# Attention with plain float32 products on parts of the array, in a pipeline one step deeper

## The chip, the cores and the metric

The kernel runs on one core of one Trainium2 chip, and the metric is the device time of one execution in microseconds (us). One core has five engines that run side by side, each through its own instructions in order: TensorE (PE; its weight loads are shown apart, as PEld), VectorE (DVE), ScalarE (ACT), GpSimd (POOL), and SyncE (SP), which issues this kernel's DMAs. [...]

## What is computed

The reference is an attention layer followed by two feed-forward layers. Only the attention is touched by the change:

```python
# q_l, k_l, v_l: 4 batches x 8 heads x 512 x 64;  q_g, k_g, v_g: 4 x 8 x 32 x 64
out_g = softmax(scale * q_g @ [k_g, k_l].T) @ [v_g, v_l]       # 32 global rows see all 544 keys
s_lg  = scale * q_l @ k_g.T                                    # local rows see the 32 global keys
s_ll  = where(abs(i - j) <= 32, scale * q_l @ k_l.T, -1e9)     # and a window of local keys
out_l = softmax([s_lg, s_ll]) @ [v_g, v_l]
...   # then x (2176 tokens x 512) through a feed-forward layer and a mixture of 8 experts
```

## The kernel before

The attention works on 16 *items*; an item is one batch and one pair of heads, so its 2 x 64 head columns fill the 128 partitions. An item has two *local steps* (`l`, two blocks of 128 queries each); after every second item comes one *global step* (`g`, the 4 x 32 global queries of two items). So five steps form a group, l l l l g, and there are 8 groups and 40 steps. A local block sees a segment of 224 keys: its own 128, the 32 global ones, and 32 from either neighbour (`SEG`).

Products are made with two float32r numbers for each float32 number: a rounded part (`hi`) and the rest (`lo`). `split_terms` makes three products of them, hi·hi, hi·lo and lo·hi, and PE adds them up in PSUM. So every operand must be split: a value leaves PSUM by an ACT copy that rounds (`hi`), and then a DVE subtraction that leaves the rest (`lo`). That is `evacuate_all` (L549 to L560).

A step goes through these pieces. `loc_scores` or `glob_scores` (PE, into two PSUM banks `s`); `loc_least` (DVE adds the mask and finds the least, from `s` to `e`) or `glob_least`; `loc_exp` or `glob_exp` (ACT; the global one reads the banks `s` themselves); `loc_normalise` (DVE reciprocal, then POOL scales `e`); `loc_transpose` or `glob_transpose` (PE turns `e` into `pta` and `ptb`), evacuated as `ah`, `al`, `bh`, `bl`; `loc_values` or `glob_values` (PE, into `pv`), evacuated into `xh`, `xl`, the input of the next layer. A global result is first scaled and picked from `pv` by four small operations (`pick`), then turned once more (`turn`).

The loop at L856 is a software pipeline written by hand, and nothing reorders it. Iteration k emits: least of step k-1, evacuation of what PE left in iteration k-1, exponentials of k-1, **values of k-4, scores of k, transposes of k-2**, then turns and the next item's `prep_qk`. Each engine gets its share of that in this order.

Operands of an item: `prep_qk` turns the raw keys and queries on PE and evacuates them to `kt` and `q`. `prep_edges` copies the neighbours' 32 columns and the global keys into `kt` by DMA (4 DMAs) and loads a later item's raw keys and queries (4 DMAs). `prep_v` splits the raw values on POOL (`split_pool`, L270) into `va`, copies edges and global values into `vb` by DMA (4 DMAs), and loads a later item's values (2 DMAs). `glob_queries` spreads the global queries with POOL copies into a block-diagonal tile `bd`, so that one 128-wide product makes the scores of two heads, the other head's rows being zeros.

During the attention `step_side` splits the first weights of the next layer on ACT, DVE and POOL, and after the last step `step_early` puts that layer's first products (L435) between the attention's last steps. From there to the end PE runs the feed-forward products (L435, L1078, L1331, L1404, L1570).

## Time and profile before

| | us |
|---|---|
| median of 3 runs (lowest, highest) | 1963.38 (1962.86, 1964.88) |
| the profiled execution, and its span | 1959.21, 1957.3 |
| PE busy | 1928.7 (99%) |
| DVE, ACT, POOL busy | 1443.9 (74%), 995.9 (51%), 581.4 (30%) |
| chain that ended last | PE 90%, DVE 3%, ACT 2%, DMA 2% |
| scores of the first and the last global step start | 23.95, 180.27 |
| first product of the next layer's second half (L1078) starts | 204.51 |

Busy shares over the whole span are those of the feed-forward layers, which last from about 205 us to the end. The attention is its first tenth, with other shares, so it has to be read by itself: in stretches from one global step to the next, and within such a stretch in the rows in order of time. A PE row's duration overlaps its neighbours' (products are pipelined), so what a block of PE work costs is read from start to start, not from durations. DMA-issuing instructions are not counted as busy.

### The profile page before, as it was taken

How to read it: one execution, taken by the hardware profiler on the slowest of the kernel's cores; microseconds unless marked ns; L12 is line 12 of the kernel's file. 1: busy time of each engine (PE TensorE's matmuls, PEld its weight loads, DVE VectorE, ACT ScalarE, POOL GpSimd, SP SyncE). 2: the span in 40 equal slices, each digit the busy share in tenths (PEclk: the TensorE clock that was granted, in tenths of full speed). 3: DMA queues.
4: the chain of work that ended last, by engine and by line, in shares of the span. 5: the costliest groups of instructions: out<-in, count | busy, mean ns of one | idle time of the engine just before them, and what ended most of it. 6: DMA issues, size and time to landing. Idle time of an engine off the chain costs nothing.

```text
span 1957.3 us, 34874 instructions
## 1 busy us (share of the span) xinstructions
PE 1928.7 (99%) x12482; PEld 1833.6 (94%) x12482; DVE 1443.9 (74%) x3075; ACT 995.9 (51%) x2325; POOL 581.4 (30%) x673
## 2 busy tenths in 40 slices
PE   9999999999999999999999999999999999999998
PEld 7888988989898899999999999999999999999998
DVE  7998575755359888888886776776777776767867
ACT  7988533323245555545554454454455454554543
POOL 6555431323126554555421101211103101111010
PEclk9999999999999999999999999999999999999999
DMA  7665220211016999998997667667676776676674
GB/s 163 139 144 133 66 65 22 65 44 49 28 32 224 308 302 301 306 301 299 311 329 269 211 224 250 214 237 244 206 260 213 248 249 236 207 258 225 208 267 141
DMA packets 359294, 391.34 MB, mean 200 GB/s; under 512 B 114256, under 2 KB 240208, under 8 KB 359120
## 3 DMA queue, kind: packets, MB, share of 16 engines
q1 hardware_dynamic: 359120, 389.10, 61.1%
q8 instruction: 99, 1.62, 0.3%
q14 instruction: 75, 0.61, 0.1%
HBM read 281.82 MB, written 96.73 MB: 193 GB/s over the span
## 4 chain that ended last, share of the span: by engine, by line
PE 90%; DVE 3%; ACT 2%; DMA 2%; SPq 1%; POOL 1%; issue 1%; DVEq 0%; POOLq 0%; ACTq 0%
PE z L1570 14%; PE a L1331 14%; PE y L1404 11%; PE h L435 10%; PE y L1078 9%; PE d L1570 7%; PE d L1331 7%; PE pa L1331 5%; PE b L1570 4%; PE b L1331 3%; PE pd L1331 2%; PE pb L1331 1%; PE pv L723 1%; ACT e L682 1%; DMA w2forms<-w 1%
## 5 line engine op out<-in xcount | busy, mean ns | idle before, releaser
L1202 POOL TENSOR_TENSOR w<-raw,w 128x256 fp32r<-128x256 f32 (+1 forms) x124 | 122.9, 1023 | 774.0 <-ACT w L1198 697.8
L1331 PE MATMUL a<-xh,w 128*128 128x384 f32 x1024 | 286.0, 335 | 0.0
L1543 ACT CAST xh<-wide 128x384 fp32r<-128x384 f32 x384 | 189.2, 512 | 112.9 <-PE d L1570 95.2
L1547 DVE TENSOR_TENSOR xl<-wide,xh 128x384 fp32r<-128x384 f32 x384 | 200.4, 549 | 24.7 <-ACT xh L1543 24.5
L1532 ACT COPY snaps<-a 128x384 f32<-128x384 f32 x128 | 61.3, 480 | 296.2 <-PE a L1331 224.8
L1404 PE MATMUL y<-w,xh 128*128 128x512 f32 x640 | 197.9, 390 | 0.7 <-ACT xh L1388 0.7
L1078 PE MATMUL y<-hid,w 128*128 128x384 f32 (+1 forms) x960 | 191.7, 356 | 0.0
L1584 DVE SCALAR_TENSOR_TENSOR acc<-z,prob,acc 128x256 f32<-128x256 f32 x366 | 162.0, 475 | 38.8 <-PE z L1570 38.7
L1331 PEld LDWEIGHTS a<-xh,w 128*128 128x128 f32 x1024 | 187.6, 188 | 0.0
L1078 PEld LDWEIGHTS y<-hid,w 128*128 128x128 f32 x960 | 171.9, 188 | 14.9
L435 PE MATMUL h<-xh,w 128*128 128x384 f32 (+1 forms) x640 | 182.6, 358 | 0.0
L1331 PE MATMUL a<-xl,w 128*128 128x384 f32 x512 | 171.2, 334 | 0.0
L1536 DVE TENSOR_TENSOR wide<-b,snaps 128x384 f32<-128x384 f32 x64 | 35.7, 557 | 157.9 <-PE b L1331 156.1
L1331 PE MATMUL d<-xh,w 128*128 128x384 f32 x512 | 150.5, 334 | 0.0
L441 ACT ACTIVATE r<-h 128x384 f32<-128x384 f32 (+1 forms) x76 | 40.4, 532 | 203.3 <-PE h L435 200.4
L1552 DVE TENSOR_TENSOR wide<-wide 128x384 f32<-128x384 f32 x256 | 138.8, 551 | 5.9 <-ACT wide L1540 0.8
L1404 PEld LDWEIGHTS y<-w,xh 128*128 128x128 f32 x640 | 119.2, 188 | 24.8 <-ACT xh L1388 1.1
L435 PEld LDWEIGHTS h<-xh,w 128*128 128x128 f32 x640 | 117.8, 188 | 13.3 <-issue 3.2
L1331 PE MATMUL pa<-xh,w 128*128 128x320 f32 x512 | 128.8, 310 | 1.0 <-ACT snaps L1366 0.6
L1404 PE MATMUL y<-w,xl 128*128 128x512 f32 x320 | 124.7, 390 | 0.9 <-DVE xl L1393 0.9
L1570 PE MATMUL z<-wf,xh 128*128 128x256 f32 x768 | 123.5, 283 | 0.0
L1540 ACT ACTIVATE wide<-wide 128x384 f32<-128x384 f32 x192 | 101.3, 528 | 33.0 <-DVE wide L1536 33.0
(255 smaller groups left out, 5073.4 us busy)
## 6 DMA issues: line engine op xcount, KB each, us to landing
raw<-in_moe_w_dram SPq DMA_DIRECT2D x128, 512.0 KB, 5.7
w<-w1forms SPq DMA_DIRECT2D x256, 256.0 KB, 4.9
w<-w2forms SPq DMA_DIRECT2D x256, 256.0 KB, 5.3
wf<-w2forms SPq DMA_DIRECT2D x192, 256.0 KB, 5.6
w1forms<-w SPq DMA_DIRECT2D x128, 256.0 KB, 4.2
w2forms<-w SPq DMA_DIRECT2D x192, 128.0 KB, 3.2
w2forms<-xl SPq DMA_DIRECT2D x64, 256.0 KB, 4.9
w2forms<-xh SPq DMA_DIRECT2D x64, 256.0 KB, 3.9
```

The costliest lines, as they stand in the source:

```text
L435: nc.tensor.matmul(ps, lhsT=w, rhs=x, start=(k == 0), stop=(k == 3 * NC - 1))
L1078: nc.tensor.matmul(ps, lhsT=w, rhs=m, start=(f == 0 and x == 0), stop=(f == last and x == 2))
L1202: eng.tensor_tensor(out=lo, in0=src, in1=f32(hi), op=ALU.subtract)
L1331: nc.tensor.matmul(ps, lhsT=lhs, rhs=rhs, start=(first and t == 0), stop=(t == 5), skip_group_check=True)
L1404: nc.tensor.matmul(y[t0], lhsT=lhs, rhs=rhs, start=(t == 0), stop=(t == 3 * UF - 1))
L1532: act.copy(snap[{"1": "p1", "5": "p5" + q, "6": "u2" + q}[i]], bank(("d" if i == "5" else "a") + q)[:, 0:n])
L1540: act.activation(out=dst, in_=bank("a" + q)[:, 0:n] if name == "A21" else dst, func=AF.Relu)
L1543: act.copy(hidden_form(name, 0, int(q)), h[HOME[name]][int(q)])
L1547: dve.tensor_tensor(out=hidden_form(name, 1, q), in0=h[HOME[name]][q], in1=f32(hidden_form(name, 0, q)), op=sub)
L1552: dve.tensor_tensor(out=x, in0=x, in1=h[other][int(q)], op=op)
L1570: nc.tensor.matmul(ps, lhsT=lhs, rhs=rhs, start=(form in ("B11", "T1") and x == 0), stop=(x == 5), skip_group_check=True)
L1584: dve.scalar_tensor_tensor(out=dst, in0=width(t, src), scalar=pr, in1=dst, op0=mul, op1=add)
```

## The change

The operands are no longer split. `kt`, `q`, `va`, `vb`, `kg`, `qg`, `vg`, `gz` and the turned probabilities (`pa`, `pb`) hold plain float32, once. PE multiplies float32 by float32, one product where there were three, and each product uses a part of the array: local scores 64 rows (as before), local values 64 columns for either head, global scores 64 rows by 32 columns, global values 32 columns. `bd` and `glob_queries` go. Values are loaded by DMA straight into `va` (two tiles for eight items each), so `split_pool` goes from `prep_v`. Copies out of PSUM are given to ACT (`"a"`) or DVE (`"v"`); only `xh`, `xl` are still split. Steps are pipelined one deeper: scores of k, values of k-5, transposes of k-3, with seven iterations after the last step instead of six.

```diff
@@ storage
-        ap3 = actx.enter_context(tc.tile_pool(name="ap3", bufs=3))
+        ap3 = actx.enter_context(tc.tile_pool(name="ap3", bufs=4))
...
+        KT = [ap1.tile([P, NQ, SEG], F32, name=f"kt{i}") for i in range(3)]
+        VA = [share.tile([P, 2, NQ, 2, P], F32, tag=f"va{i}", name=f"va{i}") for i in range(2)]
+        VB = [ap1.tile([P, NQ, P], F32, name=f"vb{i}")[0:96] for i in range(3)]
...
         def load_v(n):
...
-            r = stage.tile([P, 2, NQ, 2, D], F32, tag="r1", name="rv")[:, 0]
-            load_pair(r, v_l, b, p)
-            rawv[n] = r
+            load_pair(values_of(n).rearrange("p t (h d) -> p t h d", h=2), v_l, b, p)
@@ evacuate_all
+            for eng, hi, lo, ps, scale in waiting:
+                if eng == "a":
...
+            for eng, hi, lo, ps, scale in waiting:
+                if lo is not None:
                     nc.vector.tensor_tensor(out=lo, in0=ps, in1=f32(hi), op=ALU.subtract)
-                else:
-                    nc.vector.scalar_tensor_tensor(out=lo, in0=ps, scalar=scale, in1=f32(hi), op0=ALU.mult, op1=ALU.subtract)
+                elif eng == "v":
+                    if scale == 1.0:
+                        nc.vector.tensor_copy(hi, ps)
+                    else:
+                        nc.vector.tensor_scalar(out=hi, in0=ps, scalar1=scale, scalar2=None, op0=ALU.mult)
@@ prep_qk
-            evacuate((kt[:, 0, :, 0:P], kt[:, 1, :, 0:P], trk, 1.0))
+            evacuate(("v", kt[:, :, 0:P], None, trk, 1.0))
...
+            evacuate(("a" if n == 0 else "v", q, None, trq, QSCALE))
@@ prep_edges
-                nc.sync.dma_start(out=flat[:, 1:, 160:192], in_=flat[:, :-1, P - WINDOW : P])
-                nc.sync.dma_start(out=flat[:, :-1, 192:224], in_=flat[:, 1:, 0:WINDOW])
-                for x in range(2):
-                    nc.sync.dma_start(out=f32(kt[:, x, :, P : P + SG]), in_=keys[x])
+                nc.sync.dma_start(out=kt[:, 1:, 160:192], in_=kt[:, :-1, P - WINDOW : P])
+                nc.sync.dma_start(out=kt[:, :-1, 192:224], in_=kt[:, 1:, 0:WINDOW])
+                nc.sync.dma_start(out=kt[:, :, P : P + SG], in_=keys)
@@ prep_v
-            split_pool(va[:, 0], va[:, 1], r.rearrange("p t h d -> p t (h d)"))
...
-            for x in range(2):
-                g = vg[b * SG : (b + 1) * SG, x, p * P : (p + 1) * P]
-                nc.sync.dma_start(out=f32(vb[0:SG, x]), in_=f32(g).unsqueeze(1).to_broadcast([SG, NQ, P]))
+            g = vg[b * SG : (b + 1) * SG, p * P : (p + 1) * P]
+            nc.sync.dma_start(out=vb[0:SG], in_=g.unsqueeze(1).to_broadcast([SG, NQ, P]))
@@ loc_scores
+                for s, r in zip(s_t[i], halves):
+                    nc.tensor.matmul(s[:, t, :], lhsT=q[r, qt], rhs=kt[r, qt], start=True, stop=True)
@@ loc_transpose
-            evacuate((ah, al, pa.rearrange("p t j q -> p t (j q)"), 1.0), (bh, bl, pb[0:96].rearrange("p t j q -> p t (j q)"), 1.0))
+            evacuate(("a", a, None, pa, 1.0), ("v", c, None, pb[0:96], 1.0))
@@ loc_values
+            pv = pss.tile([P, 2, P], F32, tag="pv", name="pv")
...
+                for x, (v, e) in enumerate(zip(sources, pt)):
+                    for j, r in enumerate(halves):
+                        nc.tensor.matmul(pv[r, t], lhsT=v[:, qt, r], rhs=e[:, t, j], start=(x == 0), stop=(x == 1))
...
+            evacuate(("a", part(xh), part(xl), pv, 1.0))
@@ glob_scores
+            for x, (out, cols) in enumerate(((sa, lambda k: k[:, 0, 0 : P + SG]), (sb, lambda k: k[:, 1:NQ, 0:P]))):
+                for j, r in enumerate(halves):
+                    for y in range(2):
+                        g = slice((2 * j + y) * SG, (2 * j + y + 1) * SG)
+                        w = qg[r, p - 1 + y, b * SG : (b + 1) * SG]
+                        nc.tensor.matmul(out[g], lhsT=w, rhs=cols(KT[(n - 1 + y) % 3][r]), start=True, stop=True)
@@ glob_values
+            pv = pss.tile([P, D], F32, tag="pv", name="pv")
+            for c in range(NQ + 1):
+                for j, r in enumerate(halves):
+                    for y in range(2):
+                        g = slice((2 * j + y) * SG, (2 * j + y + 1) * SG)
...
+                        nc.tensor.matmul(pv[g], lhsT=w, rhs=v, start=(c == 0), stop=(c == NQ))
...
             def pick():
...
+                nc.vector.tensor_scalar(
+                    out=own.rearrange("p (j d) -> p j d", j=2), in0=src, scalar1=inv[:, 0:1], scalar2=None, op0=ALU.mult
+                )
@@ the loop
-        for k in range(len(steps) + 6):
+        for k in range(len(steps) + 7):
...
-            at(k - 4, loc_values, glob_values, 1)
             at(k, loc_scores, glob_scores, 1)
...
-            at(k - 2, lambda i, n, qp: loc_transpose(i), glob_transpose, 1)
+            at(k - 5, loc_values, glob_values, 1)
+            at(k - 3, lambda i, n, qp: loc_transpose(i), glob_transpose, 1)
...
-                split_pool(vg[:, 0], vg[:, 1], graw["v"])
...
-                if n % 2:
-                    glob_queries(n)
```

What that does to the order is shown at three places. On PE, a local step's iteration with a global step's transposes, before: the last two of twelve value products (L723), scores (L660), transposes (L781, L786), then the next item's keys and queries (L575, L578).

```order
L723 MATMUL pv<-bl,vb_96 128x256
L723 MATMUL pv<-bh,vb_96 128x256
L660 MATMUL s<-kt_94,q 128x224 x12
L781 MATMUL pta<-ident,e 128x128 x4
L786 MATMUL ptb<-ident,e 128x128
L575 MATMUL trk<-ident,rqk 128x128 x4
L578 MATMUL trq<-ident,rqk 128x128 x4
```

The same on PE with the change; L642 are the scores, L702 the values, L750 and L755 the transposes.

```order
L642 MATMUL s<-kt_92,q 128x224 x4
L702 MATMUL pv<-pa,va_95 64x128 x2
L702 MATMUL pv<-pb,vb_98 64x128 x2
L702 MATMUL pv<-pa,va_95 64x128 x2
L702 MATMUL pv<-pb,vb_98 64x128 x2
L750 MATMUL pta<-ident,e 128x128 x4
L755 MATMUL ptb<-ident,e 128x128
```

The scores are four products of 224 columns instead of twelve, the values eight of 128 columns instead of twelve of 256, and the values now stand behind the scores.

On ACT, the iteration that handles a global step's exponentials (L763, L764), before; L552 and L554 are evacuations.

```order
L552 CAST xh<-pv 64x256 x2
L552 CAST ah<-pta 128x512
L552 CAST bh<-ptb 96x512
L552 CAST xh<-pv 64x2x32 x2
L552 CAST kt_93<-trk 128x4x128
L554 ACTIVATE q<-trq 128x512
L763 ACTIVATE e,st<-s,st 128x160
L764 ACTIVATE e,st<-s,st 128x384
```

The same place on ACT with the change, and the iteration behind it.

```order
L551 COPY pa<-pta 128x512
L732 ACTIVATE e,st<-s,st 128x160
L733 ACTIVATE e,st<-s,st 128x384
L551 CAST xh<-pv 128x256
L551 COPY pa<-pta 128x512
L551 CAST xh<-pv 64x2x32 x2
L664 ACTIVATE e,st<-e,st 128x224 x4
L667 ACTIVATE st<-st 128x4
```

One copy stands ahead of the global exponentials instead of seven; those of `ptb`, `kt` and `q` are now DVE's, and the small ones of the turned global result have moved one iteration on.

On SP, the DMAs of one item in the steady state, before: edges and global values into `vb`, raw values, edges and global keys into `kt`, raw keys and queries.

```order
L629 DMA vb_96<-va 32x7x128
L630 DMA vb_96<-va 32x7x128
L633 DMA vb_96<-vg 32x4x128 x2
L467 DMA rv<-in_v_l_dram 128x4x64 x2
L606 DMA kt_92<-kt_92 128x7x32
L607 DMA kt_92<-kt_92 128x7x32
L609 DMA kt_92<-kg 128x4x32 x2
```

The same on SP with the change.

```order
L620 DMA vb_98<-va_96 32x3x128
L621 DMA vb_98<-va_96 32x3x128
L623 DMA vb_98<-vg 32x4x128
L467 DMA va_96<-in_v_l_dram 128x4x64 x2
L605 DMA kt_92<-kt_92 128x3x32
L606 DMA kt_92<-kt_92 128x3x32
L607 DMA kt_92<-kg 128x4x32
```

With the four loads of raw keys and queries an item has 12 DMAs instead of 14, the edge copies move 3 blocks instead of 7, and raw values go to `va` itself.

## Rows read from the trace of the kernel before

**Rows 1.** Busy time by stretch; borders are global steps' first scores (us).

```profile
core 0: us, PE busy (x) PEld busy (x) DVE busy (x) ACT busy (x) POOL busy (x), PEclk, DMA share, GB/s
23.95:44.20 20.25, 19.73 (x178) 18.25 (x177) 18.36 (x67) 18.99 (x65) 10.97 (x23) 1.00 0.73 150
...
156.56:180.27 23.71, 21.03 (x170) 18.02 (x170) 21.57 (x66) 20.51 (x67) 15.03 (x28) 1.00 0.53 127
180.27:204.51 24.24, 23.69 (x135) 20.97 (x136) 15.27 (x39) 14.13 (x40) 9.99 (x14) 0.93 0.25 81
```

**Rows 2.** PE in order of time: start, us, line, out<-in, shape, count.

```profile
101.56 0.60 PE L575 MATMUL trk<-ident,rqk 128*128 128x128 f32 x4
...
102.35 0.36 PE L723 MATMUL pv<-ah,va 128*128 128x256 f32 x1
...
103.95 0.93 PE L660 MATMUL s<-kt,q 64*128 64x224 f32 x12
104.81 0.66 PE L706 MATMUL pta<-ident,e 128*128 128x128 f32 x4
...
105.66 0.48 PE L803 MATMUL pv<-va,ah 128*128 128x256 f32 x2
...
107.61 0.93 PE L660 MATMUL s<-kt,q 64*128 64x224 f32 x12
...
111.05 0.34 PE L746 MATMUL s<-kt,bd 128*128 128x160 f32 x1
...
112.88 0.66 PE L706 MATMUL pta<-ident,e 128*128 128x128 f32 x4
```

**Rows 3.** PE in order of time, around the gate's plain float32 products (L982).

```profile
504.56 1.06 PE L982 MATMUL lt<-acc,gt 128*32 128x512 f32 x8
505.55 0.50 PE L435 MATMUL h<-xh,w 128*128 128x512 f32 x1
...
563.65 0.85 PE L982 MATMUL lt<-acc,gt 128*32 128x384 f32 x8
564.44 0.45 PE L435 MATMUL h<-xh,w 128*128 128x384 f32 x1
```

**Rows 4.** ACT by line, 23.95 to 180.27 us: xcount | busy, mean ns | idle before.

```profile
L552 ACT CAST ah<-pta 128x512 fp32r<-128x512 f32 x35 | 20.5, 586 | 9.9 <-PE pta L706 8.1 <-PE pta L781 1.3
L552 ACT CAST xh<-pv 64x256 fp32r<-64x256 f32 x56 | 20.2, 361 | 0.7 <-PE pv L723 0.3
L552 ACT CAST bh<-ptb 96x512 fp32r<-96x512 f32 x29 | 17.0, 585 | 0.0
...
L764 ACT ACTIVATE e<-s,st 128x384 f32<-128x384 f32 x7 | 4.1, 591 | 0.0
L763 ACT ACTIVATE e<-s,st 128x160 f32<-128x160 f32 x7 | 2.8, 398 | 0.0
```

**Rows 5.** DVE by line, the same stretch.

```profile
L557 DVE TENSOR_TENSOR al<-pta,ah 128x512 fp32r<-128x512 f32 x35 | 24.2, 691 | 1.1
L557 DVE TENSOR_TENSOR xl<-pv,xh 64x256 fp32r<-64x256 f32 x56 | 23.5, 419 | 1.6 <-ACT xh L552 1.2
```

**Rows 6.** SP's DMA issues in order of time, first and last of one item's.

```profile
114.99 0.92 SPq L467 DMA_DIRECT2D rqk<-in_k_l_dram  x2
...
122.48 1.35 SPq L609 DMA_DIRECT2D kt<-kg  x2
```

**Rows 7.** PE's longest waits, 23.95 to 180.27 us: total, times, longest.

```profile
PE pv L723 <- DMA vb<-vg: 3.1, 5, 1.4
...
PE s L660 <- ACT e L764: 1.4, 7, 0.2
```

**Rows 8.** PE in order of time, before the first global step.

```profile
16.79 1.07 PE L706 MATMUL pta<-ident,e 128*128 128x128 f32 x4
...
18.36 1.06 PE L575 MATMUL trk<-ident,rqk 128*128 128x128 f32 x4
...
22.42 0.36 PE L723 MATMUL pv<-ah,va 128*128 128x256 f32 x1
```

More of the change, by code (lines that the diff above doesn't have):

```diff
@@ L655, in loc_scores @@
                 qt = 2 * qp + t
-                pairs = [split_terms(q[r, 0, qt], q[r, 1, qt], kt[r, 0, qt], kt[r, 1, qt]) for r in halves]
-                for x in range(3):
-                    for s, terms in zip(s_t[i], pairs):
-                        a, c = terms[x]
-                        nc.tensor.matmul(s[:, t, :], lhsT=a, rhs=c, start=(x == 0), stop=(x == 2))
+                for s, r in zip(s_t[i], halves):
+                    nc.tensor.matmul(s[:, t, :], lhsT=q[r, qt], rhs=kt[r, qt], start=True, stop=True)
         def loc_least(i, n, qp, between):
@@ L804, in glob_values @@
             own = OG[n // 2 % 2]
             def pick():
-                for h in range(4):
-                    r = slice(h * SG, (h + 1) * SG)
-                    dst = own[r, h % 2 * D : (h % 2 + 1) * D]
-                    if h < 2:
-                        nc.scalar.activation(out=dst, in_=pv[r, h, :], func=AF.Copy, scale=inv[r, 0:1])
-                    else:
-                        nc.vector.tensor_scalar(out=dst, in0=pv[r, h, :], scalar1=inv[r, 0:1], scalar2=None, op0=ALU.mult)
+                src = pv.unsqueeze(1).to_broadcast([P, 2, D])
@@ L815, in turn @@
+                nc.vector.tensor_scalar(
+                    out=own.rearrange("p (j d) -> p j d", j=2), in0=src, scalar1=inv[:, 0:1], scalar2=None, op0=ALU.mult
+                )
             def turn():
                 ps = pss.tile([P, 2, 2, SG], F32, tag="pv", name="pv")
-                nc.tensor.transpose(ps.rearrange("p i j q -> p (i j q)"), own, ident)
+                nc.tensor.transpose(ps.rearrange("p j i q -> p (j i q)"), own, ident)
                 c0 = GL + b * SG
                 part = lambda x, r: x[r, p - 1 : p + 1, c0 : c0 + SG]
-                evacuate(*((part(xh, r), part(xl, r), ps[r, :, j, :], 1.0) for j, r in enumerate(halves)))
+                evacuate(*(("a", part(xh, r), part(xl, r), ps[r, j], 1.0) for j, r in enumerate(halves)))
```

139 lines of the change are left out of this document (48 added, 91 removed).

## The prediction

> **What bounds the kernel now.** I read the profile in this order. First the page: over the whole span PE is busy 99% and holds 90% of the chain that ended last, but these are the feed-forward layers, which the change doesn't touch. They begin at about 205 us and take the rest. So only the attention can give or take time, and what ends it earlier ends everything earlier, as long as PE stays full behind it. Then busy time by stretch, cut at the global steps [rows 1]: from the first global scores at 23.95 to the last at 180.27 us there are seven groups of five steps, (180.27 - 23.95) / 7 = **22.33 us a group**; the shortest has 20.25, the longest 23.71. In each, PE, DVE and ACT are all busy some 18 to 21.6 us. No engine alone sets the pace. [...]
>
> Last, PE in order of time, from block start to block start [rows 2]: preparing an item 102.35 - 101.56 = 0.79, local values 1.60, local scores 0.86, local transposes 0.85, global values 107.61 - 105.66 = 1.95, global scores 112.88 - 111.05 = 1.83. Eight transposes in 0.85 make 0.106 each; a global step has five and a turn, 0.64. A group has four local steps and two items: 4 x (0.86 + 1.60 + 0.85) + 2 x 0.79 + 1.83 + 1.95 + 0.64 = **19.2 us of PE work**. So PE waits 1.0 us in the shortest group and 3.1 in the mean one: for edge DMAs, for the exponentials of a global step [rows 7], for POOL and DVE.
>
> **PE after the change.** The price of plain float32 on parts of the array is in the trace already: the gate at L982 multiplies four products of 128 rows by 32 columns, side by side on the array (recorded as eight, two passes each). With 512 moving columns the block takes 505.55 - 504.56 = 0.99 us, with 384 it takes 0.79 [rows 3]. [...] The fixed part is 0.99 - 512 x 0.00156 = 0.19 us, in which the change of array layout on either side is included. So a block costs 0.19 + 0.00156 x (columns that one part has to take in series):
> - local scores, two halves abreast, 2 x 224 columns: 0.89;
> - local values, two halves abreast, 2 blocks x 2 sources x 128: 0.99;
> - global scores, four parts abreast, 160 + 384: 1.04;
> - global values, four abreast, 5 x 64: 0.69.
>
> These are chains of more and shorter pieces than the gate's; I round up to 0.95, 1.10, 1.10 and 0.85. [...] A group is then 4 x (0.95 + 1.10 + 0.85) + 2 x 0.79 + 1.10 + 0.85 + 0.64 = **15.8 us**, 3.4 less. Scores become no cheaper; values do.
>
> **ACT and DVE.** Per group ACT loses four `bh` (0.585), half of eight `xh` (0.361 each; one copy of 128 partitions takes as long as one of 64, by its columns), and two `kt` and two `q` (512 columns as well, so 0.59 each) [rows 4]: 2.3 + 1.4 + 2.4 = 6.1 off about 19.8, the mean of the two groups in [rows 1], so 13.7; the small picks and `gz` go as well, not counted. DVE loses five `al` (0.691) and half of eight `xl` (0.419) [rows 5], 5.1 us off about 20.0, so 14.9, and keeps as many 512-column operations, now copies. The trace has no such DVE copy out of PSUM; it lies between ACT's 0.585 and the subtraction's 0.691, and I take 0.6, nearer to the copy: 8 x 0.08 less, so about 14.3 us. Both come to lie under PE's 15.8, while before ACT's and DVE's 20 lay above PE's 19.2. So PE becomes the bound. POOL loses the value split and `bd`; it was busy 11 to 15 us a group [rows 1] and bounds nothing.
>
> **Waits, old and new.** Transposes of k-3 come a whole iteration after POOL has scaled `e`, so that wait goes; so does the one for `bd`, and `vb` has one step more to land. What is late next: the first local scores behind a global step. They need both banks `s`, which the global exponentials read. From the global iteration's start on PE: scores 1.10, values 0.85, half the transposes 0.43, 2.4 in all; then ACT copies `pa` (0.59) and makes the two exponentials (0.40 and 0.59, with their sums some 0.2 more) [rows 4], 4.2 us. PE's own work there is 1.10 + 0.85 + 0.85 + 0.79 = 3.6, so PE waits 0.6 and some signal time, say 0.8. Queued behind the waiting scores are values and transposes, which ACT and DVE need an iteration later. After an iteration that prepares an item DVE has `kt` and `q` to copy (1.2) before its next masks, and PE's scores stand behind these: an estimate of 0.3. That is 15.8 + 1.1 = 16.9 for an undisturbed group. Before, undisturbed was 1.0 over the PE sum and the mean 3.1; with the value split off POOL I take 1.7, so **17.5 us a group** (16.8 to 18.9 by these ends).
>
> SP: before, an item's 14 issues take 8.84 us (114.99 to 123.83), 0.63 each [rows 6]; 12 make 7.6, two items 15.2 of 17.5. It fits, but barely.
>
> **Start and end.** Until the first global step, an iteration deeper means that one block of transposes (16.79 to 18.36) and one of values (22.42 to 23.95) leave the way [rows 8, 1]: 1.57 + 1.53 = 3.1 us earlier. [...]
>
> Sum: 3.1 + 7 x (22.33 - 17.5) + 2.7 = 39.6 us. The profiled execution's own time is 1959.21 (span 1957.3 and 1.9 around it), 4.2 under the median; 1959.2 - 39.6 = 1919.6, and against the median 1963.4 - 39.6 = **1923.8 us**. With 16.8 and 18.9 us a group it is 1919 and 1934.
>
> **Rivals.**
> *SP sets the pace.* Each item's `kt` issues wait until DVE has copied `kt`, and all loads queue behind them. If SP stands there 2 us an item, a group takes 2 x (7.6 + 2) = 19.2: 3.1 + 7 x 3.1 + 2.7 = 27.5 saved, 1936. For it: 12 issues leave little room. Against it: before, too, SP filled most of its time and PE waited only 3.1 us in all for edges [rows 7], and these now have a step more.
>
> *The row halves take turns at one bank.* In the global scores both row halves write the same bank `sa`, then the same `sb`; the old local scores gave each half a bank of its own, and L982 uses all rows, so no row here shows two row parts on one bank. If they alternate, global scores cost 0.19 + 0.00156 x 2 x 544 = 1.89, 0.85 more in each of eight groups, 6.8 us: 1931. [...]
>
> *Slower: the parts don't run abreast.* If float32's two passes of one part keep the other part from starting, every block pays all its columns in series: local scores 0.19 + 896 x 0.00156 = 1.59, values 1.79, global scores 3.58, global values 2.19. A group is 4 x (1.59 + 1.79 + 0.85) + 1.58 + 3.58 + 2.19 + 0.64 = 24.9, with the same 1.7 of waits 26.6: 7 x 4.3 = 30 us more, and the end 4 us longer instead of shorter: about 1994. It decides when PE's sum passes 22.33 - 1.7 = 20.6. Against it stand the gate's rows, four abreast [rows 3]; for it only that the gate's parts share their rows and these halves partly don't.
>
> *No gain:* PE waits grow by what its work shrinks, as before, when three engines were each about 90% busy. Nothing in the sums above forces it.
>
> **How the numbers follow.** Forecast 1924 with its own range 1916 to 1934: 0.60. SP or another engine's chain at 18.9 to 20 us a group, 1934 to 1946: 0.14. The shared bank, 1931: 0.10. Fewer waits still, below 1916: 0.05. No change that can be told (0.2%, about 4 us, is what a measurement of this kernel can tell): 0.03. Slower: 0.08. The range 1911 to 1945 leaves out the slower case, no change, and the ends beyond. Faster 0.89, same 0.03, slower 0.08.
>
> **What would show it.** Right: global scores follow each other every 17 to 18 us; values start about 1.1 us before transposes, halves starting in pairs; PE's waits are small and named ACT exponentials and DVE masks; DVE and ACT busy some 14 us a group, PE nearly all of it. Wrong: score or value blocks twice as long (parts in series), global scores of 1.9 us (bank), SP without a gap and PE waiting for DMAs into `kt` or `vb`, a clock below 1.00 within groups, or gaps of PE behind 205 us, if the next layer's weights aren't ready when it starts 40 us earlier.

## The result, and the profile after

The changed kernel takes **1932.06 us** (median of 4 runs, 1930.96 to 1936.96), the kernel before beside it 1963.78 (1962.86 to 1964.88). The ratio is 0.9843, 95% interval 0.9825 to 0.9861: faster by 31.7 us. The forecast was 1924, its own range 1916 to 1934, the range on record 1911 to 1945. The profiled run took 1932.42 us, of which the span is 1930.6.

The page's first part, of the changed kernel: PE is as full as before, since most of the span is the feed-forward part.

```profile
PE 1904.1 (99%) x12714; PEld 1790.2 (93%) x12714; DVE 1400.4 (73%) x2984; ACT 948.2 (49%) x2204; POOL 542.4 (28%) x605
```

Busy time by stretch, again from one step's global scores to the next, with the columns of [rows 1]; the last row runs from the last global scores to 175 us:

```profile
core 0: us, PE busy (x) PEld busy (x) DVE busy (x) ACT busy (x) POOL busy (x), PEclk, DMA share, GB/s
19.63:36.20 16.57, 16.45 (x167) 12.48 (x166) 13.20 (x54) 13.16 (x50) 6.96 (x16) 1.00 0.64 142
36.20:53.80 17.60, 16.98 (x207) 13.17 (x206) 14.03 (x58) 13.78 (x52) 6.96 (x16) 1.00 0.65 139
53.80:74.67 20.87, 18.57 (x208) 14.32 (x207) 15.34 (x60) 14.40 (x53) 7.10 (x17) 0.92 0.64 140
74.67:92.73 18.06, 17.23 (x207) 13.17 (x206) 15.36 (x60) 14.31 (x53) 9.80 (x18) 1.00 0.50 110
92.73:111.72 18.99, 17.01 (x208) 13.18 (x207) 15.32 (x60) 14.41 (x53) 7.59 (x17) 1.00 0.71 155
111.72:130.12 18.40, 17.24 (x208) 13.17 (x207) 15.41 (x60) 14.32 (x53) 9.80 (x18) 1.00 0.59 126
130.12:150.16 20.04, 17.46 (x199) 12.82 (x199) 15.93 (x62) 16.41 (x56) 9.92 (x19) 0.99 0.70 183
150.16:175.00 24.84, 24.84 (x246) 18.63 (x247) 12.02 (x30) 11.57 (x31) 10.68 (x13) 0.94 0.07 23
```

The seven groups take (150.16 - 19.63) / 7 = 18.65 us against 22.33, and range from 16.57 to 20.87. DVE and ACT have fallen from 18.4 to 21.6 us a group to 13.2 to 16.4. PE is the fullest engine in each group, as forecast, but it is not full in all: in the third group 2.3 us are idle and the clock was 0.92.

PE in order of time (start, us, line, out<-in, shape, count), to be read from block start to block start as [rows 2]:

```profile
89.72 1.03 PE L642 MATMUL s<-kt,q 64*128 64x224 f32 x8
90.68 0.44 PE L702 MATMUL pv<-pa,va 128*64 128x128 f32 x4
...
91.71 0.66 PE L686 MATMUL pta<-ident,e 128*128 128x128 f32 x4
...
92.73 1.39 PE L716 MATMUL s<-kt,qg 64*32 64x160 f32 x16
94.05 0.65 PE L772 MATMUL pv<-va,pa 128*32 128x64 f32 x32
...
94.75 0.66 PE L686 MATMUL pta<-ident,e 128*128 128x128 f32 x4
95.24 0.60 PE L689 MATMUL ptb<-ident,e 128*96 128x128 f32 x4
95.68 0.60 PE L577 MATMUL trk<-ident,rqk 128*128 128x128 f32 x4
96.11 0.60 PE L580 MATMUL trq<-ident,rqk 128*128 128x128 f32 x4
96.64 1.41 PE L642 MATMUL s<-kt,q 64*128 64x224 f32 x8
97.98 0.33 PE L702 MATMUL pv<-pa,va 128*64 128x128 f32 x2
```

Local scores (L642) 0.96 us, local values (L702) 1.03, transposes (L686, L689) 92.73 - 91.71 = 1.02 and 95.68 - 94.75 = 0.93, global scores (L716) 1.32, global values (L772) 0.70, preparing an item (L577, L580) 0.96. The scores behind a global step, at 96.64, take 1.34.

What PE waited for in these 130.5 us (total, times, longest), beside [rows 7], and the row at their end, whose wait the list leaves out:

```profile
PE s L642 <- DMA kt<-kg: 5.1, 3, 2.2
PE s L642 <- DVE pb L559: 1.1, 2, 0.6
PE s L642 <- ACT e L732: 0.4, 2, 0.2
...
150.16 2.19 PE L716 MATMUL s<-kt,qg 64*32 64x160 f32 x16 [2.28 <-DVE st L653]
```

The gate's first block, which began at 504.56 us [rows 3], begins at 473.64, 30.9 us earlier:

```profile
473.64 1.06 PE L945 MATMUL lt<-acc,gt 128*32 128x512 f32 x8
```

It comes at a fixed place in the row of PE, so it is the clock by which all kernels below are compared: what it moves, the attention has gained or lost. Behind it the profiles scatter: span minus gate start is 1957.3 - 504.56 = 1452.7 us before and 1930.6 - 473.64 = 1457.0 after, and lies between these two or up to 0.5 above in the twelve profiles of the experiments. The spans of the profiled pair differ by 26.7 us, 4.2 less than the 30.9. With one profile of the kernel before I read these 4.2 us as scatter behind the attention, since the medians differ by 31.7.

### The profile page after: what moved, and what is told of

It reads as the page before. It is cut to its first block, busy times and chain, and to the rows that moved or that the text cites. A ratio compares the mean times of both kernels' runs of the same rounds, so it can differ in the third digit from the quotient of the medians.

```text
span 1930.6 us, 34913 instructions
## 1 busy us (share of the span) xinstructions
PE 1904.1 (99%) x12714; PEld 1790.2 (93%) x12714; DVE 1400.4 (73%) x2984; ACT 948.2 (49%) x2204; POOL 542.4 (28%) x605
## 3 DMA queue, kind: packets, MB, share of 16 engines
q8 instruction: 100, 1.64, 0.3%
## 4 chain that ended last, share of the span: by engine, by line
PE 92%; DMA 3%; DVE 2%; SPq 1%; ACT 1%; issue 1%; POOL 0%; DVEq 0%; ACTq 0%
PE z L1533 14%; PE a L1294 13%; PE y L1367 10%; PE h L435 10%; PE y L1041 10%; PE d L1533 7%; PE d L1294 7%; PE pa L1294 5%; PE b L1533 4%; PE b L1294 3%; PE pd L1294 2%; PE s L642 1%; PE pb L1294 1%; PE pv L702 1%; DMA w<-w2forms 1%; PE pta L686 1%
```

## The experiments

All go with the changed kernel unless said. "Group" is the mean of the seven stretches between global scores, "gate" the start of the gate's first block in the profile. Times are medians; the interval is that of the ratio to the kernel before, run beside each. Not all kernels ran beside each other, so kernels of different rounds are to be compared by their ratios.

| kernel | us | 95% of the ratio | group | gate |
|---|---|---|---|---|
| before (profile) | 1961.6 to 1963.8 | | 22.33 | 504.56 |
| changed (profile) | 1932.06 | 0.9825 to 0.9861 | 18.65 | 473.64 |
| again | 1934.79 | 0.9840 to 0.9884 | 19.03 | 477.38 |
| weights_r1 | 1926.93 | 0.9803 to 0.9838 | 17.83 | 468.56 |
| values_queue_pool | 1931.46 | 0.9819 to 0.9852 | 18.17 | 473.46 |
| values_in_turn | 1938.20 | 0.9866 to 0.9908 | 19.66 | 481.50 |
| gscores_halves_r1 | 1927.99 | 0.9807 to 0.9836 | 18.08 | 470.04 |
| depth_4_2 | 1934.63 | 0.9833 to 0.9881 | 19.35 | 479.89 |
| depth_4_2_r1 | 1924.32 | 0.9789 to 0.9818 | 17.68 | 467.05 |
| before_depth_5_3 | 2017.09 | 1.0232 to 1.0314 | 28.75 | 550.41 |
| three_e (one run) | 1961.07 | | 22.74 | 504.05 |
| values_first_r1 | 1927.61 | 0.9802 to 0.9829 | 18.58 | 473.77 |
| values_first_r1_abs | 1922.94 | 0.9781 to 0.9808 | 17.60 | 467.19 |
| mixed_r1_abs | 1921.75 | 0.9783 to 0.9810 | 17.50 | 465.27 |

**again**: no edit.

> The changed kernel once more, with a profile of its own. In its first profile the feed-forward gave back 4.4 us of the 30.9 us that the attention had gained: the clock fell to 0.5 at 549.1 to 552.5 us behind the 1.88 us wait for DVE's acc, and two later waits were 0.5 to 0.7 us longer each. Theory: these are chance, not a consequence of the change; then this profile shows the first feed-forward product about 31 us earlier than in the kernel before, as the first one did, but the clock drop at 549 us and the longer waits need not be there, and the span may be 1926 to 1931 us. Rival: the attention's new end shifts the feed-forward's transfers against its work; then the same drop at the same place comes again, and the span is 1930 to 1931 us.

The gate moved 27.2 us this time, 30.9 in the first profile: the waits for `kt` were 6.6 us instead of 5.1, and waits for DVE's masks came to 2.4, where the first profile's list has none (2.3 more stand in both before the last global scores). So much the attention itself varies from one execution to the next; neither span that was expected came, 1933.9 was measured. The clock drop behind the 1.88 us wait is there again (0.57 over the 3 us behind it). Over all fourteen profiles it stands in nine, and not in those of the kernel before, depth_4_2, values_in_turn, values_first_r1 and mixed_r1_abs, of which four have the change's products. The stretch in which it falls, in the first profile and in that of mixed_r1_abs, each with the stretch ahead of it, in which PE is idle 3.00 - 1.12 = 1.88 us (columns as above):

```profile
546.64:549.64 3.00, 1.12 (x7) 1.07 (x6) 3.00 (x7) 1.09 (x3) 1.87 (x2) 0.92 0.00 0
549.64:552.64 3.00, 3.00 (x15) 1.50 (x14) 1.42 (x3) 2.04 (x6) 2.22 (x3) 0.52 0.84 307
```

```profile
538.27:541.27 3.00, 1.12 (x11) 0.93 (x14) 3.00 (x7) 1.09 (x3) 1.87 (x2) 1.00 0.00 0
541.27:544.27 3.00, 3.00 (x26) 2.38 (x25) 1.41 (x3) 3.00 (x9) 2.35 (x3) 1.00 0.84 307
```

It comes and goes behind the same wait, so the theory was right that the change doesn't bring it, and wrong in taking it for an exception.

**weights_r1** and **values_queue_pool**: who makes PE wait for the key edges?

```diff
-                    load_part(0, EARLY_PARTS[n], tag="r0")
+                    load_part(0, EARLY_PARTS[n], tag="r1")
```

> One edit to the changed kernel: the two early raw weight loads go into the stage buffer r1, which nothing uses by then, instead of taking one of the two r0 buffers that the raw queries and keys turn over in. Theory (buffer rotation): with r0 taken, SP waits at 54.9 and at 94.0 us until a later item's transposes have run, then issues 12 DMAs back to back, and the key edges land at 67.4 and 106.0 us, after PE wanted them; that is 2.24 and 1.92 us of PE waits for kt, and the clock drop at 67.86 us behind the first costs about 1.7 us more. Without the conflict these go: the groups that took 20.87 and 18.99 us come to about 17.5, and the kernel is 5 to 7 us faster, about 1926 us. Rival (SP's issues set the pace, 12 of some 0.63 us an item): the count is the same, the edges stay late, and the time moves by less than 1.5 us.

```diff
-        def load_pair(dst, src, b, p):
+        def load_pair(dst, src, b, p, queue=nc.sync):
...
-                nc.sync.dma_start(...)
+                queue.dma_start(...)
...
-            load_pair(values_of(n)..., v_l, b, p)
+            load_pair(values_of(n)..., v_l, b, p, nc.gpsimd if n > 1 else nc.sync)
```

> The changed kernel with the loads of the values (two DMAs an item, from the third item on) issued by POOL instead of SP; the early weight loads keep taking an r0 buffer. SP then issues 10 DMAs an item instead of 12, about 6.3 us instead of 7.6. Theory (buffer rotation): SP still stands at 54.9 and 94.0 us until a later item's transposes, but has 1.2 to 2.4 us less to issue behind it, so the kt waits (5.1 us in the first profile, 6.6 in the second) fall by about half, and the time falls by 2 to 4 us to about 1930 us, less than the r1 buffer gave (1926.9). Rival (SP's count of issues): the waits go altogether and the time falls as with the r1 buffer or more, to 1927 us or below.

SP's queue in order of time, first of the changed kernel:

```profile
54.91 0.57 SPq L361 DMA_DIRECT2D raw<-in_moe_w_in_dram  x1
57.81 0.92 SPq L467 DMA_DIRECT2D rqk<-in_k_l_dram  x2
...
63.25 1.20 SPq L605 DMA_DIRECT2D kt<-kt  x1
64.49 0.65 SPq L606 DMA_DIRECT2D kt<-kt  x1
65.18 0.63 SPq L607 DMA_DIRECT2D kt<-kg  x1
```

and the product on PE that these feed, with its wait in brackets, and the two behind it:

```profile
67.41 1.47 PE L642 MATMUL s<-kt,q 64*128 64x224 f32 x8 [2.24 <-DMA kt<-kg]
68.81 0.69 PE L702 MATMUL pv<-pa,va 128*64 128x128 f32 x4
...
70.71 0.91 PE L750 MATMUL pta<-ident,e 128*128 128x128 f32 x4
```

Between the early weight load at 54.91 and the next raw load at 57.81 SP stands still: both `r0` buffers are taken, one by the weights. The twelve issues behind run back to back, the last edge is issued at 65.18, and PE, which wanted it at 67.41 - 2.24 = 65.17, waits. Behind the wait PE's granted clock was 0.50 from 67.86 to 71.27 us: local values take 70.71 - 68.81 = 1.90 us there, not 1.03. With `r1` the same place reads:

```profile
55.03 0.63 SPq L361 DMA_DIRECT2D raw<-in_moe_w_in_dram  x1
55.76 1.00 SPq L467 DMA_DIRECT2D rqk<-in_k_l_dram  x2
...
64.45 0.59 SPq L607 DMA_DIRECT2D kt<-kg  x1
...
66.79 1.03 PE L642 MATMUL s<-kt,q 64*128 64x224 f32 x8 [1.33 <-DMA kt<-kg]
```

The stand is gone, the clock stays at 1.00, waits for `kt` fall from 5.1 (6.6) to 1.3 us, the third and fifth group from 20.87 and 18.99 to 18.12 and 17.82, and the kernel from 1934.8 to 1926.9 us, 7.9 less by the runs beside it. By the ratios it is 0.9820 against 0.9862, or against 0.9843 in the first round, which would be 4.5 us; so the buffer is worth some 5 to 8 us. Buffer rotation was the cause of most of the waits; but one wait of 1.33 us stays with SP nearly always busy there, so the count of issues has a share. That is what values_queue_pool says too: with two issues an item fewer but the conflict kept, the waits for `kt` come to 3.3 us in three times, the third group to 17.96 and the time to 1931.5. As the theory put it, it gave less than the buffer. Its ratio, 0.9836, can't be told from the changed kernel's 0.9843, and its gate hides the shorter groups, since its first global scores came 2.3 us later (21.96 against 19.63).

**values_in_turn**: the two heads' values one behind the other.

```diff
-            for t in range(2):
-                qt = 2 * qp + t
-                for x, (v, e) in enumerate(zip(sources, pt)):
-                    for j, r in enumerate(halves):
+            for j, r in enumerate(halves):
+                for t in range(2):
+                    qt = 2 * qp + t
+                    for x, (v, e) in enumerate(zip(sources, pt)):
```

> The changed kernel with the local values' two heads, which lie on the two halves of the array's columns, issued one after the other (all four products of the first head, then all four of the second) instead of in pairs. Theory: products on different parts run abreast only when they stand next to each other in PE's row; a block of local values goes from 1.03 us to about 1.7 us (1.79 by the sum of its products one by one), 0.7 us in each of 32 blocks, and since PE is what the attention waits for, most of it arrives at the end: 15 to 23 us more, 1947 to 1955 us. Rival: the parts were never abreast in a way that matters, or PE has spare time; then the block stays at 1.03 us or the time moves by less than 4 us.

The block goes to 1.52 us, less than 1.7: the first passes stand 0.11 us apart, a single part at work, and then the second head's products start beside the rest of the first head's, pairs 0.055 apart. The gate comes 4.1 us later than in `again` and 7.9 later than in the first profile, for 32 x 0.49 = 15.7 us of added blocks. PE's busy time between the global scores rose from 120.9 to 132.1 us, but the waits for `kt` fell to 3.4 us and most others went: half the added work or more lies where PE had waited. By the runs beside it the time moved by 3.4 us only, which is the rival's second figure (PE has time to spare, less than 4 us). So the second head's products do run abreast and save PE time, and PE is the bound, but a soft one while SP and the buffers hold it up now and then. The expected 15 to 23 us was too much for both reasons, the block's price and the waits that it filled.

**gscores_halves_r1**: do row halves at one bank take turns?

```diff
-            for x, (out, cols) in enumerate(((sa, ...), (sb, ...))):
-                for j, r in enumerate(halves):
+            for j, r in enumerate(halves):
+                for out, cols in ((sa, ...), (sb, ...)):
                     for y in range(2):
```

> The changed kernel with the early weight loads in r1 and the global scores' loops turned round: both banks for the first row half (head 0 of each pair), then both banks for the second, instead of both row halves at the first bank and then both at the second. With r1 alone a block of global scores took 1.05 to 1.32 us, its four parts starting 6 to 7 ns apart at one bank. Theory (the row halves work abreast at one bank): turned round they stand behind each other in PE's row and mostly take turns: 0.19 + 0.00156 x (160 + 384 + 384) = 1.64 us or up to 1.89, some 0.6 us more in each of eight blocks, 3 to 6 us more in all, about 1930 to 1933 us. [...]

The time is that of weights_r1, 1927.99 against 1926.93 us, and not the theory's 1930 to 1933. Row halves that take turns in either order would leave it there as well, but that is not the reason. In the order as it was, the four parts of a block start within 20 ns (57.394, 57.401, 57.408, 57.414 us in depth_4_2_r1), all at one bank, both row halves among them, and a block takes 1.05 us when nothing holds it: 0.19 + 0.00156 x 544 = 1.04, the sum's raw figure. So the halves don't take turns. Turned round, three of the eight blocks take 1.06 to 1.11, not 1.64: the second half's products on the first bank start 0.067 us behind the first half's, ahead of those on the second bank that stand before them in the row. Four others take 1.59 to 1.75 and one 2.65: there the first product into the second bank starts 0.38 us late (54.78 us, behind one at 54.40), and the second half's follow only behind it, at 54.79. In the changed kernel's trace the weight load for that bank waits 0.38 us for DVE's masks (at 93.27 us); that the late start here is the same wait is my estimate, and it was not shown.

**depth_4_2**, **depth_4_2_r1**, **before_depth_5_3**, **three_e**: what is the depth worth?

```diff
+            at(k - 4, loc_values, glob_values, 1)
             at(k, loc_scores, glob_scores, 1)
...
-            at(k - 5, loc_values, glob_values, 1)
-            at(k - 3, lambda i, n, qp: loc_transpose(i), glob_transpose, 1)
+            at(k - 2, lambda i, n, qp: loc_transpose(i), glob_transpose, 1)
```

with `range(len(steps) + 6)`; depth_4_2_r1 has the line of weights_r1 as well, and before_depth_5_3 is the reverse edit in the kernel before.

> The changed kernel with the order of the kernel before: a step's values come four steps after its scores, ahead of the new scores, and its probabilities are turned two steps after; the float32 products on parts of the array stay. Theory: the gain is mostly PE work that is gone (19.2 us a group before, 15.8 us by the sum), and the deeper order only takes the waits of PE for exp, mask and copies. Then this kernel keeps most of the gain but waits more: 18.65 us a group becomes about 19.5 to 21, that is 6 to 18 us more than the changed kernel, 1938 to 1950 us. Rival: PE work alone is worth little without the depth, since ACT and DVE set the pace; then the groups stay near 22.3 us and the time near 1960 us.

> The changed kernel with the old order (values four steps after the scores and ahead of the new scores, turns two steps after) and with the two early weight loads in r1. With the old order alone the groups were 16.23, 16.34, 22.40, 16.97, 23.32, 16.73 and 23.46 us: the long ones are those in which PE waits 2.7 and 3.1 us for vb at 65.26 and 104.98 us (and 2 to 3 us more go in the slow clock behind them). Theory: both waits come from the r0 conflict, and the deeper order's PE blocks cost more than the old order's (global scores 1.32 against 1.05 us), so the depth itself buys nothing; then the two groups come to about 17 us, the attention is 12 us shorter than with the old order alone, and the time is about 1921 to 1926 us, at or under that of the deeper order with r1 (1926.9). Rival: the depth is needed for vb to land in time, whatever the buffer; then PE keeps waiting 2 to 3 us for vb and the time stays near 1932 us.

> The kernel before with the deeper order alone: values five steps after the scores and behind the new scores, turns three steps after, one iteration more at the end; the products stay split in three. (The e buffers stay three, since a fourth doesn't fit beside the split tiles.) Theory: before, PE had 19.2 us of work a group, ACT and DVE about 20, so waits that the deeper order removes on PE are taken by ACT and DVE; the group goes from 22.33 us to no less than 21, and the time moves by -9 to +4 us against the kernel before, 1953 to 1966 us. Rival (the order is what the change gains by): the waits for POOL e, bd and vb go, the groups come to about 20 us, and the time to about 1945 us.

The new products in the old order are as fast as the changed kernel, better than expected: 1934.63 beside 1934.79 us. Its groups are 16.23, 16.34, 22.40, 16.97, 23.32, 16.73 and 23.46 us. PE's longest waits there, 23.47 to 158.92 us, and then with r1, 23.20 to 146.96:

```profile
PE pv L702 <- DMA vb<-vg: 5.8, 2, 3.1
PE pta L686 <- POOL e L674: 2.8, 5, 1.2
```

```profile
PE pta L686 <- POOL e L674: 2.9, 5, 1.1
PE pv L702 <- DMA vb<-vg: 1.7, 2, 1.4
```

The depth does what it says: the waits for POOL's `e` are there at two steps and gone at three, and `vb` lands later than PE wants it. But the big ones were SP's stand again, at the values instead of the scores, and r1 takes most of them. Then the old order needs 17.68 us a group against 17.83, and 1924.32 us against 1926.93, with intervals that overlap. **The depth by itself is worth nothing that can be told here**; the gain is that of the rest of the change: the float32 products, the copies and loads that go with them, and the fourth `e` buffer, which both kernels of the old order kept. These were not taken apart. The rival of depth_4_2, that PE's work is worth little without the depth, falls.

In the kernel before the deeper order costs 54 us, which neither the theory (1953 to 1966) nor the rival had. DVE's longest waits there say why:

```profile
DVE e L671 <- PE pv L817: 24.6, 6, 5.1
DVE e L671 <- PE ptb L709: 17.5, 9, 3.5
```

With three `e` buffers DVE may write a step's masked scores only when PE has got through the transposes of three steps before. So this run was no clean test of the order, and the changed kernel was given three as well:

```diff
-        ap3 = actx.enter_context(tc.tile_pool(name="ap3", bufs=4))
+        ap3 = actx.enter_context(tc.tile_pool(name="ap3", bufs=3))
```

> The changed kernel with three buffers for the exponentials e and the sums st instead of four. The kernel before, given the deeper order with its three buffers, took 2017 us, with 29 us a group, and its DVE stood 17.5 us for PE's turns of e and 24.6 for PE's values. Theory: the loss there was the missing fourth buffer, not the order; then this kernel loses as well, since DVE may write the masks of a step only when PE has turned the step three before: groups of 22 to 26 us instead of 18.65, 30 to 50 us more, 1960 to 1985 us. Rival: three are enough and the order cost the old kernel its time in another way; then it stays within 4 us of 1933.

It falls back to 22.74 us a group and 1961 us, with PE standing 11.1 us at local and 6.7 us at global scores for DVE's masks up to 146 us:

```profile
PE s L642 <- DVE st L653: 11.1, 17, 1.3
PE s L716 <- DVE st L653: 6.7, 12, 0.9
```

So without the fourth buffer, one number of the diff, the deeper order's kernel has no gain left that can be told (one run, 2.1 us under the kernel before beside it). What the deeper order does to the kernel before with four buffers, and what the old order does in the changed kernel with three, wasn't tried and stays open.

**values_first_r1**, **values_first_r1_abs**, **mixed_r1_abs**: can the rest be had?

```diff
+            at(k - 5, loc_values, glob_values, 1)
             at(k, loc_scores, glob_scores, 1)
...
-            at(k - 5, loc_values, glob_values, 1)
```

> The changed kernel with r1 for the early weight loads and one line moved: the values of five steps ago are issued ahead of the new scores instead of behind them; the turns stay three steps behind. Theory: what the deeper order lost in PE blocks is the place of the values, not the depth. With the scores first, the local scores behind a global step take 1.33 us instead of 0.96 and a block of global scores 1.24 to 1.32 instead of 1.05, since the second of the two score banks comes free late and no block of values stands ahead to cover that; with the values first (old order with r1) both had 0.96 and 1.05 and the undisturbed groups 16.34 to 16.44 us. So this kernel should have 1.05 and 0.96 there and groups of 16.3 to 16.9, without the waits for POOL e (2.9 us) that the shallower turns left: the attention ends 4 to 7 us earlier than with r1 alone, about 1920 to 1924 us. Rival: the block prices come from the change of array layout between neighbouring blocks, which the depth fixes, not the order; then global scores stay at 1.2 us and more and the time at 1926 to 1928 us.

The block prices came as expected: 1.05 for global and 0.96 for local scores, also behind a global step. But a new wait took the gain, from 20 to 146 us:

```profile
PE pv L702 <- DVE xl L556: 9.1, 6, 3.9
```

Values and turns share two PSUM banks (`m`). Behind each turn of the global outputs the values now need the bank that the values of the iteration before filled, since the turn has taken the other: at 43.66 us they begin behind DVE's `xl` of those values (43.09 to 43.51), while the `xl` of the turn itself begins only at 44.03. So the expectation of mixed_r1_abs, that the turn's own bank is waited for, names the wrong one. With the scores first, these had stood between. The time is that of weights_r1, the rival's figure, but the block prices were the theory's.

```diff
+            if k == len(steps) - 2:
+                step_side(1)
             at(k - 1, loc_exp, glob_exp)
...
-                step_side((3 if kind == "g" else 1) if n < 14 else 3)
+                step_side((3 if kind == "g" else 1) if n < 14 else 2 if k == len(steps) - 2 else 3)
```

> The same, and in the last iteration but one ACT's first pass over the raw weights is issued ahead of that iteration's exponentials instead of behind them. Theory: in the last group DVE stood 2.7 us for that pass (ACT reached it after four exponentials), and PE then 2.3 us for DVE's masks before the last global scores; that wait goes and the last group falls from about 19 to 17 us, 1.5 to 2.5 us less than without. Rival: the exponentials that come 0.7 us later hold PE back as much, or the copies on ACT do; within 1 us of the kernel without.

In the changed kernel DVE stood in the last group for ACT's pass over the raw weights, which ACT reached only behind four exponentials:

```profile
147.39 0.66 ACT L289 ACTIVATE cv<-raw 128x512 f32<-128x512 f32 x1
...
148.08 0.43 DVE L291 TENSOR_SCALAR cv<-cv 128x512 uint32<-128x512 uint32 x1 [2.70 <-ACT cv L289]
```

Issued earlier, the wait of the last global scores falls from 1.96 us in values_first_r1 to 0.73 us, and the last group from 22.99 to 18.79; 4.7 us less by the runs, more than the 2.5 expected, since the wait for `xl` in that group fell as well, from 3.85 to 2.45.

```diff
-            at(k - 5, loc_values, glob_values, 1)
-            at(k, loc_scores, glob_scores, 1)
+            orders = [(k - 5, loc_values, glob_values, 1), (k, loc_scores, glob_scores, 1)]
+            for o in reversed(orders) if turned else orders:
+                at(*o)
+            turned = bool(due)
```

> The kernel with r1, the values first and ACT's pass over the raw weights moved, and one more edit: in the iteration after a turn of the global outputs the scores go ahead of the values again. Theory: with the values first PE stood 1.0 to 1.1 us in each group (2.4 us in the last) at the values behind a turn, since these need the bank m that the turn had just filled and that ACT and DVE had not emptied; a block of scores in between (0.96 us) covers that, as in the changed kernel. So six waits of 7.7 us in all go nearly whole, the groups come to 16.4 to 16.7 us, and the time falls from 1922.9 by 5 to 7 us to 1916 to 1918 us, the least of all kernels here. Rival: the scores that come first there wait for their own bank s (as behind a global step, 0.27 to 0.38 us) and DVE's masks come later, so that half the gain or more is taken back: 1919 to 1922 us.

The waits for `xl` are gone, the blocks' medians are at their least, and five groups take 16.97 to 17.28 us. What is left of PE's waits, from 20 to 146 us:

```profile
PE s L642 <- DMA kt<-kg: 1.6, 1, 1.6
PE s L716 <- DVE st L653: 1.4, 3, 0.7
PE s L642 <- DVE st L653: 1.1, 2, 0.9
```

1921.75 us is the least of all, but with 0.9797 of the kernel before against 0.9795 it can't be told from values_first_r1_abs: the rival's figure, not the theory's 1916 to 1918. The group came to 17.50, not 16.4 to 16.7; of the 7.7 us of waits that went, the gate shows 1.9. Most of the rest is where the rival put it: the six blocks of local scores behind a turn, now first again, take 1.57 to 1.83 us instead of 0.96.

## Why the prediction was right, and where its sizes were off

**PE becomes the bound: right in kind.** DVE and ACT fell below PE, by nearly the amounts forecast (ACT 13.7 against 13.2 to 14.4 in the first six groups, DVE 14.3 against 13.2 to 15.4). ACT's `xh` copy of 128 partitions takes 368 ns where that of 64 took 361. The price law taken from the gate, 0.19 us + 0.00156 us a column of one part, has its slope from the two blocks of [rows 3], (0.99 - 0.79) / 128. That the four parts run abreast is in their starts, 504.558 to 504.578 us; what one part costs alone no row of the kernel before shows, and values_in_turn does: 0.11 us a pass of 128 columns, so with two passes 0.0017 us a column. The law held to 0.07 us for raw blocks: local scores 0.89 and 0.96 measured, local values 0.99 and 1.03, global scores 1.04 and 1.05 when undisturbed, global values 0.69 and 0.70. The rounding up was needed for the first alone. What the sum missed are the hand-overs behind the transposes: I carried 0.85 us a block and 0.79 an item over from [rows 2], and they take 0.93 to 1.02 and 0.97. With the measured prices a group is 4 x (0.96 + 1.03 + 0.93) + 2 x 0.97 + 1.05 + 0.70 + 0.69 + 0.20 = 16.3 us, 0.5 over the 15.8. The transposes themselves got no dearer; what follows them sets their price. In the kernel before, four of them take 0.36 us up to a product on the whole array and 0.44 up to another transpose:

```profile
108.96 0.60 PE L709 MATMUL ptb<-ident,e 128*96 128x128 f32 x4
109.32 0.37 PE L723 MATMUL pv<-ah,va 128*128 128x256 f32 x1
...
113.37 0.60 PE L709 MATMUL ptb<-ident,e 128*96 128x128 f32 x4
113.81 0.27 PE L817 MATMUL pv<-ident,og 128*128 128x128 f32 x1
```

In the changed kernel they take the same 0.44 up to another transpose (95.24 to 95.68 above), the same 0.36 up to a product on the whole array (153.87 to 154.23), and 0.53 up to a product on parts (92.20 to 92.73); the medians of 0.44 and 0.53 are the same in every profile in which the case occurs. In [rows 2] products on the whole array followed, now scores on parts or other transposes do. The prediction took its 0.19 us to hold the change of array layout on either side. It doesn't: the product just ahead of the gate's block takes 504.56 - 504.24 = 0.32 us where those before it take 0.23, so 0.09 us fall on the neighbour, and the sum had no term for them.

**Undisturbed waits, 1.1 us a group: right, in part for other reasons.** The second group of weights_r1, with no wait over 0.3 us in it, takes 17.39, 1.1 above 16.3. Scores behind the global step hold 0.38 of it (forecast 0.8), another block of local scores 0.31, an item's preparation 0.17, and the global scores 0.19, where the sum had no wait.

**Disturbed waits, 0.6 us a group on top: the step that failed.** 18.65 - 17.4 = 1.25 where 0.6 was put down. "It fits, but barely" was counted over whole items, 15.2 of 17.5 us; it didn't ask whether SP may begin its issues. It may not, twice, because a raw weight load sits in one of the two buffers through which queries and keys pass, and then twelve issues in a row come late, and behind the first of the two waits the clock falls to 0.50. Not all of the 1.25 is SP's: PE's 2.28 us before the last global scores are a wait for DVE's masks, which r1 leaves as it was (2.35). The rival "SP sets the pace" had the right queue, and the wrong cause: with the buffer changed alone, some 5 to 8 us came. The same line stands in the source of the kernel before; there PE asked for two items' edges in 22.33 us instead of 18.65, and what the conflict cost it was not tried.

**Start and end.** The first global scores came 23.95 - 19.63 = 4.3 us earlier, not 3.1 (3.7 to 3.8 in weights_r1 and again). The end gained 30.9 - (180.27 - 150.16) = 0.8 us, not 2.7. The 2.7 was my estimate: a sum of PE work at a granted clock of 1.00 against the last row of [rows 1], where it is 0.93. It rests on a price for the next layer's first products that no run shows; in the changed kernel the 48 of them that stand between the attention's last steps take 11.9 us from start to start (in six blocks, 154.23 to 173.91 us), 0.23 us each where they follow one another. The granted clock is 0.94 after the change, so no slow stretch went away. PE is busy for all of the 24.84 us, so it wasn't the iterations waiting for each other.

So: 4.3 + 7 x (22.33 - 18.65) + 0.8 = 30.9 us in place of 39.6, of which seven groups of 1.15 us are 8.1, start and end together 0.7.

**The rivals.** *The row halves take turns at one bank*, 1931 us: the nearest to the measured time, by luck. Its block was to be 1.89 us; 1.32 was measured in the changed kernel, and 1.05 wherever the second bank was free in time. Two row halves of 64 rows wrote one bank with starts 6 to 7 ns apart and at the price of work abreast, so these tiles don't take turns at it. *Parts don't run abreast*: global scores were to take 3.58 us and took 1.32. *SP sets the pace*: above. *No gain*: PE's idle time between the first and the last global scores did not grow but fell, from 156.32 - 143.54 = 12.8 us to 130.53 - 120.94 = 9.6.

**What the prediction did not see**: that the depth is worth nothing that can be told here. Its terms "transposes come a whole iteration after POOL" and "`vb` has one step more" are true (2.8 to 2.9 us of POOL waits come back without them), but the scores, issued ahead of the values, lose as much at their banks: 1.33 us behind a global step where values ahead of them make it 0.96. A wait that is removed at one block can be paid at its neighbour; the run with the old order tells what the balance is, and a profile of the kernel before doesn't.

## What to carry to other kernels

When work on the fullest engine shrinks by a sixth, list every buffer that two kinds of transfers share, and ask for each issue queue not only whether its issues fit but what each issue must wait for: here one tag on a load was worth 5 to 8 us beside a gain of 31.7. A block's price read from start to start leaves out what the block does to the one ahead of it: look at the neighbour too, and at what will follow after the change. An order that removes a wait should be weighed together with the block that it moves forward, whose own buffer may come free later. And a deeper pipeline lives by its buffers: with three instead of four the same order gave everything back.

## What the runs showed of the hardware that was not expected

- Plain float32 products on four parts of 64 rows by 32 columns, two row halves of them into one PSUM bank, took 1.05 us where nothing held them; 0.19 us + 0.00156 us a column of one part, the law of the gate's parts, gives 1.04.
- By the records' starts, a product whose part was free began ahead of earlier ones whose part was busy: with the loops turned round (gscores_halves_r1), the second row half began 0.067 us behind the first although two products of the first stood between. With four products of one part ahead (values_in_turn), the second part began only some 0.5 us later.
- Four float32 transposes took 0.36 us up to a product on the whole array, 0.44 up to another transpose and 0.53 up to a product on parts, in the kernels with the old products and with the new.
- The granted clock fell to 0.50 behind a PE wait of 2.24 us and stayed at 1.00 behind one of 1.33 us at the same place; behind a wait of 1.88 us, the same in all kernels, it fell in nine of fourteen profiles, to 0.50 to 0.58 over 3 us, and not in five. The length of a wait alone doesn't tell: the clock stayed at 1.00 behind one of 2.45 us in values_first_r1_abs (134.76 us) and one of 2.08 in `again` (107.83), and in before_depth_5_3 it fell at 86.36 us, where the longest wait of the 9 us before was 1.55 (85.17).
